# From the third chunk on, VectorE transposes gates, k and q in 32x32 squares

## The chip, the cores and the metric

The kernel runs on one core of a Trainium2 chip. The metric is the device time of one execution in microseconds (us); the time of a kernel is the median of its runs.

## The reference

A gated linear attention (HGRN2) feeds a SwiGLU block. Batch is 4, heads 8, sequence 768, head size 48; the block has 3072 tokens, width 384 and hidden width 1536, all float32.

```python
f = 1.0 / (1.0 + np.exp(-f_logit))
for t in range(S):
    state = f[:, :, t, :, None] * state + np.einsum('bhd,bhe->bhde', k[:, :, t], v[:, :, t])
    y[:, :, t] = np.einsum('bhd,bhde->bhe', q[:, :, t], state)
x = y.transpose(0, 2, 1, 3).reshape(B * S, H * D)
g = x @ w_gate
return (g * (1.0 / (1.0 + np.exp(-g))) * (x @ w_val)) @ w_out
```

## The kernel before

`short_path` does all the work; `general_path` is a second version behind a flag, which runs only when gates become too small. The sequence is cut into six chunks of 128 tokens. A unit is one batch entry of one chunk, so there are 24 units, four to a chunk.

**Attention of a unit** (`attention`, line 453) is a generator whose steps are given out one by one. Tokens arrive on the partitions: f, k and q of 128 tokens and 8 heads lie in `raw` buffers, two for each tensor (lines 332 to 336), each head padded from 48 to 64 columns, so that two heads make 128 columns. The computation wants channels on the partitions and tokens along the free dimension. `transposed` (line 458) therefore has TensorE transpose four 128x128 pieces of a tensor, one for each pair of heads, into one PSUM bank. The steps are:

- f is transposed; ScalarE takes the sigmoid out of PSUM into `gate` (466).
- VectorE scans the gates backwards into `tail` (471), keeps the smallest whole-chunk decay in `least` (474) and prepares `start` (475, 476).
- k and q are transposed; VectorE multiplies k by the tails into `kT` (482), scans forwards into `head` (484) and multiplies q by it into `qT` (486). GpSimd makes the decayed state (490), and `load_after` asks for the unit two further on.
- TensorE forms the scores `sc` (498), VectorE masks them (500), and kT is transposed back into `kt` (505, 507).
- TensorE forms the output `y` from the decayed state (519) and from the scores (522). ScalarE copies it (526), and ten small DMAs on SyncE's queue place it in `xT` (532). `dS` (544) updates the state (550).

**The block** of chunk 0 is a plain product. For chunks 1 to 5, `mlp_seven` (685) does it with Strassen's seven products: first token sums of xT on VectorE, then six `pair` pieces (products on line 715, in four PSUM banks of pool `fps`, whose sums and products VectorE forms on lines 658, 731 and 746), then four down-projection pieces (line 779).

**Order.** `take_turns` gives out the pieces of a chunk's block and between them the 16 attention parts of the next chunk (`attention_steps`, 567). Thus attention of chunks 2 to 5 runs beside the blocks of chunks 1 to 4, and chunk 5's block runs alone. A scheduler then orders each engine's instructions, earlier written first where they are ready; inside a pair TensorE's order is written out (`in_order`). Loads go on SyncE's queue, one DMA each for f, k, q and v of a unit, and so do the copies into xT. SyncE, like the engines, takes its instructions in order. `judge` (946) reduces `least` to the flag that picks the path.

Of the kernel before, what the change touches and what calls it, by code (L numbers as in the profile page):

```python
# [9 lines left out]
FP32 = mybir.dt.float32  # L10
I32 = mybir.dt.int32
U32 = mybir.dt.uint32
AF = mybir.ActivationFunctionType
ALU = mybir.AluOpType
# [5 lines left out]
def general_path(ctx, tc, q, k, v, f_logit, moe_w_gate, moe_w_val, moe_w_out, out):  # L20
# [14 lines left out]
    NCH = S // C  # L35
    HP = H // 2
    W = 64
# [84 lines left out]

    states = [const.tile([128, HP, 2, D], FP32, tag=f"state{i}", name=f"state{i}") for i in range(3)]
    for s in states:
# [7 lines left out]
    def attention(u):  # L132
# [4 lines left out]
        def transposed(dst, src):  # L137
            for a in range(HP):
                nc.tensor.transpose(dst[:, a * C:(a + 1) * C],
                                    src[:, 2 * a:2 * a + 2, :].rearrange("t r d -> t (r d)"), ident)  # L140
# [3 lines left out]
        transposed(p[:, 1], kr)  # L144
        fT = att.tile([128, HP, C], FP32, tag="e1", name="fT")
        nc.scalar.copy(fT, p[:, 0].rearrange("p (a t) -> p a t", t=C))
        kT = att.tile([128, HP, C], FP32, tag="kT", name="kT")
        nc.vector.tensor_copy(kT, p[:, 1].rearrange("p (a t) -> p a t", t=C))
        p = aps.tile([128, 2, 512], FP32, tag="a", name="qTp")
        transposed(p[:, 0], qr)  # L150
        q0 = att.tile([128, HP, C], FP32, tag="q0", name="q0")
        nc.scalar.copy(q0, p[:, 0].rearrange("p (a t) -> p a t", t=C))
# [137 lines left out]
def short_path(ctx, tc, ident, least, judge, q, k, v, f_logit, moe_w_gate, moe_w_val, moe_w_out, out):  # L290
# [9 lines left out]
    nc = tc.nc  # L300
    B, H, S, D = q.shape
    C = 128
    NCH = S // C
    HP = H // 2
    W = 64
# [5 lines left out]
    N1 = C + 1  # L311
    NRAW = 2
    NROT = 2
    assert TB <= 512 and DM % 128 == 0 and D <= W

    const = ctx.enter_context(tc.tile_pool(name="const", bufs=1))
    att = ctx.enter_context(tc.tile_pool(name="att", bufs=1))
# [11 lines left out]
                            pattern=[[1, C]], channel_multiplier=-1)  # L329


    raw = {nm: [const.tile([128, H, W], FP32, tag=f"{nm}raw{i}", name=f"{nm}raw{i}") for i in range(NRAW)]
           for nm in "qkf"}
    for nm in "fkq":
        for t in raw[nm]:
# [3 lines left out]

    gates = [const.tile([128, HP * N1 + 2], FP32, tag=f"gates{i}", name=f"gates{i}") for i in range(NROT)]  # L340
    tails = [const.tile([128, HP * N1 + 2], FP32, tag=f"tails{i}", name=f"tails{i}") for i in range(NROT)]
    start = const.tile([128, HP * N1], FP32, tag="start", name="start")
# [11 lines left out]
    def pairs(t, off=0):  # L354
        return t[:, off:off + HP * N1].rearrange("p (a t) -> p a t", t=N1)
# [17 lines left out]
    units = [(b, c) for c in range(NCH) for b in range(B)]  # L373
    vt = {}

    def load(u):
        b, c = units[u]
        rows = slice(c * C, (c + 1) * C)
        for nm, src in (("f", f_logit), ("k", k), ("q", q)):
            nc.sync.dma_start(out=raw[nm][u % NRAW][:, :, 0:D], in_=src[b, :, rows, :].rearrange("h t d -> t h d"))  # L380
        vt[u] = att.tile([128, H, D], FP32, tag="v", name="v", bufs=4)
        nc.sync.dma_start(out=vt[u], in_=v[b, :, rows, :].rearrange("h t d -> t h d"))
# [67 lines left out]
    def bank(name):  # L450
        return aps.tile([128, 512], FP32, tag="a", name=name)

    def attention(u):
        b, c = units[u]
        fr, kr, qr = (raw[nm][u % NRAW] for nm in "fkq")
        gate, tail = (x[u % NROT] for x in (gates, tails))

        def transposed(name, src):
            p = bank(name)
            for a in range(HP):  # L460
                nc.tensor.transpose(p[:, a * C:(a + 1) * C],  # L461
                                    src[:, 2 * a:2 * a + 2, :].rearrange("t r d -> t (r d)"), ident)
            return p.rearrange("p (a t) -> p a t", t=C)

        p = transposed("fTp", fr)
        nc.scalar.activation(pairs(gate)[:, :, 1:N1], p, AF.Sigmoid)  # L466
        yield


        n = HP * N1  # L470
# [5 lines left out]
        nc.vector.reciprocal(pairs(start)[:, :, 0:1], pairs(start)[:, :, 0:1])  # L476
        yield

        kp = transposed("kTp", kr)
        qp = transposed("qTp", qr)  # L480
        kT = att.tile([128, HP, C], FP32, tag="kT", name="kT")
        nc.vector.tensor_tensor(kT, kp, pairs(tail, 2)[:, :, 0:C], ALU.mult)
        head = att.tile([128, n], FP32, tag="head", name="head", bufs=1)
        nc.vector.tensor_tensor_scan(head, gate[:, 0:n], start, 1.0, op0=ALU.mult, op1=ALU.add)
        qT = att.tile([128, HP, C], FP32, tag="qT", name="qT")
        nc.vector.tensor_tensor(qT, qp, pairs(head)[:, :, 1:N1], ALU.mult)
        if c:
            load_after(u)
            decayed = att.tile([128, HP, 2, D], FP32, tag="decayed", name="decayed")
            nc.gpsimd.tensor_tensor(decayed, states[b], whole.unsqueeze(2).broadcast_to((128, HP, 2, D)), ALU.mult)  # L490
        yield
# [10 lines left out]
        if c < NCH - 1:  # L502
            p = bank("kt")
# [9 lines left out]
        if c:  # L513
# [13 lines left out]
            for h in range(H):  # L527
                f = h * D
                while f < (h + 1) * D:
                    n = min((h + 1) * D, (f // 128 + 1) * 128) - f  # L530
                    r = W * (h % 2) + f - h * D
                    nc.sync.dma_start(out=xT[c][f % 128:f % 128 + n, f // 128, b * C:(b + 1) * C],
                                      in_=yT[r:r + n, h // 2, :])
# [7 lines left out]
        if c < NCH - 1:  # L541
            p = bank("dS")
            for h in range(H):
                nc.tensor.matmul(p[W * (h % 2):W * (h % 2) + W, (h // 2) * D:(h // 2 + 1) * D],  # L544
                                 lhsT=kt[:, h, :], rhs=vt[u][:, h, :], start=True, stop=True)
            dS = p[:, 0:HP * D].rearrange("p (a d) -> p a d", d=D)
            for par in range(2):
                half = slice(W * par, W * par + W)
                if c:
                    nc.vector.tensor_tensor(states[b][half, :, par, :], decayed[half, :, par, :], dS[half], ALU.add)  # L550
                else:
                    nc.scalar.copy(states[b][half, :, par, :], dS[half])
# [3 lines left out]
        if not c:  # L556
            p = bank("xTp")
# [3 lines left out]
        yield  # L561

    def load_after(u):
        if u + NRAW < len(units):
            load(u + NRAW)

    def attention_steps(c):

        runs = [attention(c * B + b) for b in range(B)]
        parts = [1, 2, 1, 2]  # L570
        order = sorted((2 * b + s, b, n) for b in range(B) for s, n in enumerate(parts))
        return [lambda b=b, n=n: [next(runs[b]) for _ in range(n)] for _, b, n in order]
# [284 lines left out]
    for u in range(NRAW):  # L857
        load(u)
    mark = traced[-1]
    keep_warm(5)  # L860
    first = [attention(b) for b in range(B)]
    done = [0] * B

# [6 lines left out]
    fetches.pop(0)()  # L870
    run(0, 0, 1, 2)
    load_after(0)
    for b in range(1, B):
        if b == 1:
            run(1, 0)
            keep_warm(12)
        run(b, 1)
        run(b - 1, 3)
        run(b, 2)
        load_after(b)  # L880
        if b == 1:
            for _ in range(2):
                fetches.pop(0)()
        if b + 1 < B:
            run(b + 1, 0)
        else:
            sizes.pop(0)()
        if b > 1:
            run(b - 2, 5)
        run(b - 1, 4)  # L890
# [31 lines left out]
@with_exitstack  # L922
def kernel(
    ctx: ExitStack,
    tc: tile.TileContext,
    q: bass.AP,
    k: bass.AP,
    v: bass.AP,
    f_logit: bass.AP,
    moe_w_gate: bass.AP,  # L930
    moe_w_val: bass.AP,
    moe_w_out: bass.AP,
    out: bass.AP,
):


    nc = tc.nc
    args = (q, k, v, f_logit, moe_w_gate, moe_w_val, moe_w_out, out)
    HP = q.shape[1] // 2
    flags = ctx.enter_context(tc.tile_pool(name="flags", bufs=1))  # L940
    least = flags.tile([128, HP], FP32, tag="least", name="least")
    ident = flags.tile([128, 128], FP32, tag="idf", name="idf")
    make_identity(nc, ident)
    redo = []

    def judge(bank):
        low = flags.tile([128, 1], FP32, tag="low", name="low")
        nc.vector.tensor_reduce(low, least, axis=mybir.AxisListType.X, op=ALU.min)
        row = bank("row")[0:1, 0:128]
        nc.tensor.transpose(row, low, ident)  # L950
        one = flags.tile([1, 1], FP32, tag="one", name="one")
        nc.vector.tensor_reduce(one, row, axis=mybir.AxisListType.X, op=ALU.min)
        flag = flags.tile([1, 1], I32, tag="flag", name="flag")
        nc.vector.tensor_single_scalar(flag, one, LEAST, op=ALU.is_lt)
        redo.append(nc.values_load(flag[0:1, 0:1], min_val=0, max_val=1,
                                   skip_runtime_bounds_check_because="a comparison"))

    short_path(tc, ident, least, judge, *args)
    with tc.If(redo[0] > 0):
        general_path(tc, *args)  # L960
# [32 lines left out]
```

## Time and profile before

| | |
|---|---|
| median of 3 runs | 671.41 us (671.12 to 671.87) |
| the profiled execution | 671.64 us, its span 669.9 us |
| TensorE busy | 657.1 us (98%) |
| VectorE busy | 443.5 us (66%) |
| ScalarE busy | 191.5 us (29%) |
| GpSimd busy | 22.5 us (3%) |
| TensorE line 461, transposes of f, k and q | 3 x 96 |
| DMA packets | 120667, of them 103712 under 512 bytes |
| moved by DMA | 42.47 MB |

The span is the time from the first to the last instruction in the profiled execution. In lines of the timeline the first number is the start in us from the span's start, the second the length; a line may stand for several instructions that overlap or follow each other (x and a count). The figure in brackets is the engine's idle time before the line and what ended it. In a table by stretch, each engine has its busy time in that stretch. PE is TensorE's matmul, PEld its weight load, DVE VectorE, ACT ScalarE, POOL GpSimd, SPq SyncE's queue.

### The profile page before, as it was taken

Reading aid. Unit: us, or ns where it says so; the run is one execution under the profiler, and the core shown is the slowest. Engines: PE = TensorE matmul, PEld = TensorE weight load, DVE = VectorE, ACT = ScalarE, POOL = GpSimd, SP = SyncE. Lnnn points to the kernel's source line nnn. Section 1 sums busy time; section 2 is a strip of 40 time slices with the busy share of each in tenths; the row PEclk is TensorE's granted clock in tenths of the full one; section 3 lists DMA queues with packets and bytes.
Section 4 is the critical chain, followed back from the end, with each engine's and each line's share of the span. In section 5 each row is a group of like instructions: output and inputs, shape, how many; then the busy total and the mean of one; then the engine's idle time right before and its main releaser. Section 6 shows DMA issues by size and latency. Waiting matters only on the chain.

```text
span 669.9 us, 10567 instructions
## 1 busy us (share of the span) xinstructions
PE 657.1 (98%) x4206; PEld 550.0 (82%) x4206; DVE 443.5 (66%) x765; ACT 191.5 (29%) x284; POOL 22.5 (3%) x38
## 2 busy tenths in 40 slices
PE   7999998999999999999999999999999999999996
PEld 5955555658888999888899888899988898988896
DVE  6889688687778626686843877762587772366631
ACT  2566546203332311323311334131141421111110
POOL 2000000000000000000000000000000000000000
PEclk9999999999999999999999999999999999999999
DMA  9976638113112032121221221212211000100001
GB/s 205 217 196 208 167 106 238 34 24 82 36 36 49 13 64 68 36 48 22 50 46 51 59 48 25 48 28 53 64 39 33 12 1 13 62 1 0 1 1 51
DMA packets 120667, 42.47 MB, mean 63 GB/s; under 512 B 103712, under 2 KB 114464, under 8 KB 120608
## 3 DMA queue, kind: packets, MB, share of 16 engines
q1 hardware_dynamic: 117152, 36.98, 23.7%
q10 hardware_dynamic: 3456, 4.72, 2.0%
q8 instruction: 35, 0.57, 0.4%
q14 instruction: 24, 0.20, 0.1%
HBM read 33.03 MB, written 4.72 MB: 56 GB/s over the span
## 4 chain that ended last, share of the span: by engine, by line
PE 82%; DVE 2%; DMA 1%; issue 0%; ACT 0%; ACTq 0%
PE p L715 31%; PE o L779 21%; PE c L715 12%; PE o L626 4%; PE y L519 3%; PE sc L498 3%; PE y L522 2%; PE kTp L461 1%; PE dS L544 1%; PE kt L505 1%; PE qTp L461 1%; PE fTp L461 1%; DMA w<-in_moe_w_out_dram 1%; DVE top L417 0%; DVE h L618 0%
## 5 line engine op out<-in xcount | busy, mean ns | idle before, releaser
L658 DVE TENSOR_TENSOR rest<-u,p 128x512 f32<-128x512 f32 x90 | 61.8, 687 | 59.8 <-PE p L715 59.6
L779 PE MATMUL o<-w_out,h 128*128 128x192 f32 x480 | 83.6, 329 | 0.0
L779 PEld LDWEIGHTS o<-w_out,h 128*128 128x128 f32 x480 | 77.7, 190 | 2.3 <-issue 1.1
L715 PE MATMUL p<-xT,w_gate 128*128 128x256 f32 x240 | 71.4, 379 | 0.0
L715 PE MATMUL p<-xT,w_val 128*128 128x256 f32 x240 | 71.4, 379 | 0.0
L658 DVE TENSOR_TENSOR u<-u,p 128x512 f32<-128x512 f32 x90 | 61.5, 683 | 5.7 <-PE p L715 1.7
L745 ACT ACTIVATE h<-rest 128x768 f32<-128x768 f32 x30 | 25.3, 843 | 121.5 <-DVE rest L658 121.4
L715 PE MATMUL c<-xT,w_gate 128*128 128x256 f32 x180 | 54.6, 385 | 0.0
L715 PE MATMUL c<-xT,w_val 128*128 128x256 f32 x180 | 53.5, 379 | 0.0
L715 PEld LDWEIGHTS p<-xT,w_val 128*128 128x128 f32 x240 | 45.6, 190 | 6.2
L715 PEld LDWEIGHTS p<-xT,w_gate 128*128 128x128 f32 x240 | 45.6, 190 | 6.2
L658 DVE TENSOR_TENSOR u<-u,o 128x384 f32<-128x384 f32 x15 | 8.3, 555 | 48.9 <-PE o L779 48.9
L715 PEld LDWEIGHTS c<-xT,w_val 128*128 128x128 f32 x180 | 34.2, 190 | 4.6
L471 DVE TENSOR_TENSOR_SCAN tails<-gates,ones 128x516 f32<-128x516 f32 x24 | 29.5, 1230 | 11.9 <-ACT gates L466 11.9
L490 POOL TENSOR_TENSOR decayed<-state,tails 128x384 f32<-128x384 f32 x20 | 19.1, 954 | 532.7 <-DVE state L550 284.8
L715 PE MATMUL p<-xs,sv 128*128 128x256 f32 x120 | 35.8, 380 | 0.0
L715 PE MATMUL p<-xs,sg 128*128 128x256 f32 x120 | 35.7, 379 | 0.0
L500 DVE TENSOR_TENSOR A<-sc,causal 128x512 f32<-128x512 f32 x48 | 31.3, 684 | 5.9 <-PE sc L498 5.8
L522 PE MATMUL y<-A,v 128*48 128x128 f32 x320 | 34.8, 274 | 0.0
L519 PE MATMUL y<-qT,decayed 128*48 128x128 f32 x320 | 34.8, 278 | 0.0
L715 PEld LDWEIGHTS c<-xT,w_gate 128*128 128x128 f32 x180 | 31.5, 190 | 3.9 <-ACT u L723 0.2
L466 ACT ACTIVATE gates<-fTp 128x512 f32<-128x512 f32 x24 | 14.3, 597 | 70.5 <-PE fTp L461 69.5
(117 smaller groups left out, 1116.2 us busy)
## 6 DMA issues: line engine op xcount, KB each, us to landing
fraw<-in_f_logit_dram SPq DMA_DIRECT2D x24, 192.0 KB, 3.0
kraw<-in_k_dram SPq DMA_DIRECT2D x24, 192.0 KB, 3.0
qraw<-in_q_dram SPq DMA_DIRECT2D x24, 192.0 KB, 3.4
v<-in_v_dram SPq DMA_DIRECT2D x24, 192.0 KB, 2.9
w<-in_moe_w_gate_dram SPq DMA_DIRECT2D x6, 768.0 KB, 4.5
w<-in_moe_w_val_dram SPq DMA_DIRECT2D x6, 768.0 KB, 4.5
w<-in_moe_w_out_dram SPq DMA_DIRECT2D x6, 768.0 KB, 5.4
out_dram<-ob ACTq DMA_DIRECT2D x24, 192.0 KB, 2.1
```

Of the source, the lines that this page charges most:

```text
L461: nc.tensor.transpose(p[:, a * C:(a + 1) * C], src[:, 2 * a:2 * a + 2, :].rearrange("t r d -> t (r d)"), ident)
L471: nc.vector.tensor_tensor_scan(tail[:, 0:n][:, ::-1], gate[:, 0:n][:, ::-1], ones[:, ::-1], 1.0, op0=ALU.mult, op1=ALU.add)
L490: nc.gpsimd.tensor_tensor(decayed, states[b], whole.unsqueeze(2).broadcast_to((128, HP, 2, D)), ALU.mult)
L498: nc.tensor.matmul(sc[par][:, a * C:(a + 1) * C], lhsT=kT[r, a, :], rhs=qT[r, a, :], start=True, stop=True)
L500: nc.vector.tensor_tensor(A[:, par], sc[par].rearrange("p (a t) -> p a t", t=C), causal.unsqueeze(1).broadcast_to((128, HP, C)), ALU.mult)
L519: nc.tensor.matmul(y[rows_of(par), cols], lhsT=decayed[:, a, par, :], rhs=qT[:, a, :], start=True, stop=False, skip_group_check=True)
L522: nc.tensor.matmul(y[rows_of(par), cols], lhsT=vt[u][:, 2 * a + par, :], rhs=A[:, par, a, :], start=False, stop=True, skip_group_check=True)
L626: nc.tensor.matmul(p, lhsT=h[n // 2][:, n % 2 * 2 + b // 2, b % 2 * C:(b % 2 + 1) * C], rhs=w_out[:, j, :], start=(n == 0), stop=(n == NF ...
L658: nc.vector.tensor_tensor(dst, a, b, ALU.add)
L715: nc.tensor.matmul(p[:, n, :], lhsT=lhsT, rhs=rhs, start=first and n == 0, stop=last, skip_group_check=True)
L745: nc.scalar.activation(h[j][:, 1:4, :], rest[:, :, 0, :], AF.Silu)
L779: nc.tensor.matmul(p[:, n, :], lhsT=lhsTs[j][:, n * C:(n + 1) * C], rhs=rhs[:, j, :], start=first and j == 0 and n == 0, stop=last and j = ...
```

## The change

For units of chunks 2 to 5 (`c >= SQUARES`), f, k and q are not transposed on TensorE. Instead of one DMA, four bring each tensor in, one for each group of 32 partitions: partition t of a group gets tokens 4t to 4t + 3, all 48 channels, for the four heads of one parity (768 consecutive bytes of a head). For the groups that hold channels 32 to 47 the destination starts 32 columns earlier, so that the same columns hold the wanted 32 channels in all groups; the upper 16 of these are other data, which later steps don't read or meet with zeros. ScalarE takes the sigmoid in place, and VectorE's transpose turns each 32x32 square and writes its 32 tokens with a step of four words. For k and q this goes to `kT` and `qT`, and the products on lines 482 and 486 then work in place there. The two buffers of a tensor become one tile, `rooms`; a squares load takes up most of both, so it is issued only after the transposes of the unit before. Smaller edits keep the padding rows out of the state update and the verdict.

```diff
+    SQUARES = 2
...
-    raw = {nm: [const.tile([128, H, W], FP32, tag=f"{nm}raw{i}", name=f"{nm}raw{i}") for i in range(NRAW)]
+    rooms = {nm: const.tile([128, NRAW * H * W], FP32, tag=f"{nm}raw", name=f"{nm}raw") for nm in "qkf"}
+    raw = {nm: [rooms[nm][:, i * H * W:(i + 1) * H * W].rearrange("t (h d) -> t h d", d=W) for i in range(NRAW)]
            for nm in "qkf"}
...
+    Q = 32
+    NI = C // Q
+    RUN = NI * D
+
+    def squares(nm):
+        return rooms[nm][:, Q:Q + HP * RUN].rearrange("t (a i e) -> t a i e", a=HP, i=NI)[:, :, :, 0:Q]
+
+    def in_turn(t):
+
+        return t.rearrange("p a (t i) -> p a i t", i=NI)
+
     def load(u):
...
         for nm, src in (("f", f_logit), ("k", k), ("q", q)):
+            if c >= SQUARES:
+                for n in range(4):
+                    at = Q * (1 - n % 2)
+                    nc.sync.dma_start(
+                        out=rooms[nm][Q * n:Q * (n + 1), at:at + HP * RUN].rearrange("t (a e) -> t a e", a=HP),
+                        in_=src[b, n // 2::2, rows, :].rearrange("a (t i) d -> t a (i d)", i=NI))
+                continue
...
-        p = transposed("fTp", fr)
-        nc.scalar.activation(pairs(gate)[:, :, 1:N1], p, AF.Sigmoid)
+        if c >= SQUARES:
+            nc.scalar.activation(squares("f"), squares("f"), AF.Sigmoid)
+            nc.vector.transpose(in_turn(pairs(gate)[:, :, 1:N1]), squares("f"))
+        else:
+            p = transposed("fTp", fr)
+            nc.scalar.activation(pairs(gate)[:, :, 1:N1], p, AF.Sigmoid)
...
+        qT = att.tile([128, HP, C], FP32, tag="qT", name="qT")
+        if c >= SQUARES:
+            kp, qp = kT, qT
+            nc.vector.transpose(in_turn(kT), squares("k"))
+            nc.vector.transpose(in_turn(qT), squares("q"))
+            load_after(u)
+        else:
+            kp = transposed("kTp", kr)
+            qp = transposed("qTp", qr)
...
-                half = slice(W * par, W * par + W)
+                half = rows_of(par)
...
     def load_after(u):
-        if u + NRAW < len(units):
-            load(u + NRAW)
+
+        for w, ahead in ((u + 1, True), (u + 2, False)):
+            if w < len(units) and (units[w][1] >= SQUARES) == ahead:
+                load(w)
...
-        nc.vector.tensor_reduce(one, row, axis=mybir.AxisListType.X, op=ALU.min)
+        nc.vector.tensor_reduce(one, row.rearrange("p (n d) -> p n d", n=2)[:, :, 0:D], axis=mybir.AxisListType.XY, op=ALU.min)
```

More of the change, by code (lines that the diff above doesn't have):

```diff
@@ L477, in attention @@
         yield
-        kp = transposed("kTp", kr)
-        qp = transposed("qTp", qr)
         kT = att.tile([128, HP, C], FP32, tag="kT", name="kT")
+        qT = att.tile([128, HP, C], FP32, tag="qT", name="qT")
[7 more added lines that the diff above has]
+            qp = transposed("qTp", qr)
         nc.vector.tensor_tensor(kT, kp, pairs(tail, 2)[:, :, 0:C], ALU.mult)
@@ L484, in attention @@
         nc.vector.tensor_tensor_scan(head, gate[:, 0:n], start, 1.0, op0=ALU.mult, op1=ALU.add)
-        qT = att.tile([128, HP, C], FP32, tag="qT", name="qT")
         nc.vector.tensor_tensor(qT, qp, pairs(head)[:, :, 1:N1], ALU.mult)
         if c:
-            load_after(u)
+            if c < SQUARES:
+                load_after(u)
             decayed = att.tile([128, HP, 2, D], FP32, tag="decayed", name="decayed")
@@ L938 @@
     args = (q, k, v, f_logit, moe_w_gate, moe_w_val, moe_w_out, out)
-    HP = q.shape[1] // 2
+    HP, D = q.shape[1] // 2, q.shape[3]
     flags = ctx.enter_context(tc.tile_pool(name="flags", bufs=1))
```

## The prediction

> **What bounds the kernel now.** I read the page first: its header, the busy shares, the slices and the chain that ended last.
>
> ```profile
> span 669.9 us, 10567 instructions
> ...
> PE 657.1 (98%) x4206; PEld 550.0 (82%) x4206; DVE 443.5 (66%) x765; ACT 191.5 (29%) x284; POOL 22.5 (3%) x38
> ...
> PE   7999998999999999999999999999999999999996
> ...
> PEclk9999999999999999999999999999999999999999
> ...
> PE 82%; DVE 2%; DMA 1%; issue 0%; ACT 0%; ACTq 0%
> ```
>
> TensorE is busy in every slice, at an unreduced granted clock, and the chain runs along it: 82% of the span, against 2% on VectorE. A busy TensorE could still hide waits, so next I read the busy time by stretch: one whole chunk period from its first hidden pair to the next one's, and the last period, in which no attention runs.
>
> ```profile
> core 0: us, PE busy (x) PEld busy (x) DVE busy (x) ACT busy (x) POOL busy (x), PEclk, DMA share, GB/s
> ...
> 259.60:367.50 107.90, 107.90 (x754) 96.96 (x753) 70.50 (x127) 28.57 (x42) 3.33 (x4) 1.00 0.21 45
> ...
> 579.40:669.90 90.50, 84.47 (x432) 77.14 (x431) 44.82 (x81) 12.55 (x21) 0.00 (x0) 0.99 0.04 15
> ```
>
> TensorE is covered for 107.90 of 107.90 us, VectorE for 70.50. In the last period TensorE's busy time is 84.47 us, so four attention units cost the period 107.90 - 84.47 = 23.4 us, 5.9 us a unit. Third, who TensorE's weight loads wait for between 151 and 580 us:
>
> ```profile
> PEld y L519 <- issue: 4.3, 19, 0.3
> ...
> PEld sc L498 <- DVE qT L486: 2.3, 7, 0.3
> ```
>
> The longest entries come to a few us in 428 and none is a single wait over 0.3 us. In the periods that the change touches, TensorE waits for nobody: work taken off it shortens the span, as long as VectorE, which gets the work, doesn't make it wait.
>
> **What leaves TensorE.** Chunks 2 to 5 are 16 units, each with twelve 128x128 transposes (line 461). The timeline gives the distance from one start to the next, which counts where operations overlap:
>
> ```profile
> 259.06 0.60 PE L461 MATMUL fTp<-idf,fraw 128*128 128x128 f32 x4
> ...
> 259.50 0.60 PE L715 MATMUL c<-xT,w_gate 128*128 128x256 f32 x2
> ...
> 269.00 0.60 PE L461 MATMUL kTp<-idf,kraw 128*128 128x128 f32 x4
> ...
> 269.43 0.60 PE L461 MATMUL qTp<-idf,qraw 128*128 128x128 f32 x4
> ...
> 269.87 0.60 PE L715 MATMUL c<-xT,w_gate 128*128 128x256 f32 x2
> ```
>
> Four transposes take 0.44 us, then 0.87 for eight: 1.31 us a unit, 16 x 1.31 = 21.0 us. The four periods' busy time of that line, overlaps counted, is the other bound:
>
> ```profile
> sum 427.60, PE 26.75 PEld 21.96; mean PE 6.69 PEld 5.49
> ```
>
> So the term is -21.0 to -26.8 us. I take -21.6 (1.35 a unit), close to the lower end, because the starts in the timeline are what the next matmul sees; the 0.04 a unit over them stands for the two changes of operands that go as well.
>
> **What VectorE gets.** Three transposes of 128x512 f32 a unit, 48 in all; no such operation is in the trace. The nearest rows are element-wise operations of VectorE with unit stride, by shape and then in sequence:
>
> ```profile
> L658 DVE TENSOR_TENSOR rest<-u,p 128x512 f32<-128x512 f32 x90 | 61.8, 687 | 59.8 <-PE p L715 59.6
> ...
> L658 DVE TENSOR_TENSOR hs<-h 128x256 f32<-128x256 f32 x30 | 12.6, 419 | 0.4
> ```
>
> ```profile
> 269.20 0.69 DVE L658 TENSOR_TENSOR rest<-u,p 128x512 f32<-128x512 f32 x1 [1.04 <-PE p L715]
> 269.80 0.68 DVE L482 TENSOR_TENSOR kT<-kTp,tails 128x512 f32<-128x512 f32 x1
> 270.40 0.68 DVE L486 TENSOR_TENSOR qT<-qTp,head 128x512 f32<-128x512 f32 x1
> ```
>
> An operation of 512 elements lasts 0.69 us and holds the engine 0.60; from 256 to 512 elements it grows by 0.27, or 1.05 ns an element, so 128 elements would last 0.29. I take 0.62 us of engine time for a transpose, the row of the same size. It could come out near 1.2: the transpose writes every fourth word (tokens four to a partition), and a slope of twice 1.05 ns over 512 elements adds 0.54 us. It would also be about that if it were cut into four operations of 128 elements (4 x 0.29 us). So 0.6 to 1.2 us. The Trainium skill's page SBUF — State Buffer, section Door 1: The DMA port swizzle, says that an engine's stream needs two hits to a 16-byte line for full rate and that each access in a new line pays a penalty; by it this write would be on the slow side, and no row of this case shows it. The time that would follow is the second rival, worked out from the rows.
>
> Where does this work lie? The two halves of a period, pairs then down projections, and the fullest stretch I found:
>
> ```profile
> 259.50:331.10 71.60, 71.60 (x460) 62.44 (x459) 54.44 (x94) 22.60 (x33) 2.50 (x3) 1.00 0.20 42
> 331.10:367.50 36.40, 36.40 (x297) 34.62 (x297) 16.16 (x34) 5.96 (x10) 0.83 (x1) 1.00 0.22 50
> ```
>
> ```profile
> 282.00:292.50 10.50, 10.50 (x87) 9.46 (x83) 9.31 (x17) 4.43 (x7) 0.83 (x1) 1.00 0.28 57
> ```
>
> In the down stretch VectorE is 44% busy and hides what comes. The pair stretch holds three units' worth: VectorE goes to 54.4 + 9 x 0.62 = 60.0 us, TensorE to 71.6 - 3 x 1.35 = 67.5, a load of 89%. The 10.5 us stretch has 9.31 / 10.50 = 89% already, and TensorE is covered throughout: such a load can be borne. What a lag costs is seen at the tightest place in that stretch, where, as I count the pairs' four banks, one product must be read before TensorE can begin a later one:
>
> ```profile
> 288.25 0.69 DVE L658 TENSOR_TENSOR u<-u,p 128x512 f32<-128x512 f32 x1
> ```
>
> ```profile
> 289.75 0.59 PE L715 MATMUL p<-xT,sg 128*128 128x256 f32 x2
> ```
>
> The bank is free at 288.94 and wanted at 289.75: 0.81 us to spare. After the change TensorE comes up to 1.35 us earlier and VectorE up to 3 x 0.62 = 1.86 later, so the wait is between nothing and 1.35 + 1.86 - 0.81 = 2.4 us a unit; over 12 units, 0 to 29 us. I take 3 us in all (0.25 a unit), near the lower end, for two rows. Gates no longer wait for TensorE, and ready work is moved forward by the scheduler: the verdict's reduction, written after chunk 4's last step (about 579 us), ran at 548.59. And VectorE has regular gaps to fill:
>
> ```profile
> 548.59 0.16 DVE L948 TENSOR_REDUCE low<-least 128x1 f32<-128x4 f32 x1
> ```
>
> ```profile
> DVE rest L658 <- PE p L715: 46.5, 66, 1.0
> ```
>
> Between 151 and 580 us these are 66 waits of 0.70 us on average, one transpose of 0.62 each.
>
> **The small edits.** The sigmoid takes as many elements from SBUF instead of PSUM; ScalarE is 29% busy, so nothing. Its old reason to wait goes for 16 of 24 units:
>
> ```profile
> ACT gates L466 <- PE fTp L461: 69.5, 15, 11.2
> ```
>
> What is late next for it is the load, and for the transposes VectorE's own queue. The products kT and qT now read two SBUF tensors, and the trace shows what that can cost beside GpSimd:
>
> ```profile
> 261.73 0.83 POOL L490 TENSOR_TENSOR decayed<-state,tails 128x384 f32<-128x384 f32 x1 [26.00 <-DVE tails L471]
> ...
> 262.09 1.56 DVE L484 TENSOR_TENSOR_SCAN head<-gates,start 128x516 f32<-128x516 f32 x1
> ```
>
> ```profile
> 308.60 1.23 DVE L484 TENSOR_TENSOR_SCAN head<-gates,start 128x516 f32<-128x516 f32 x1
> ```
>
> The scan lasts 1.56 us where GpSimd's product starts just before it and 1.23 where none runs: +0.33. At worst each of 16 units pays one such meeting, 5.3 us of VectorE time, and none at best; it counts within the 3 us. The Trainium skill's page SBUF — State Buffer, section SBUF: two separate sides, states that a VectorE operation with two SBUF inputs and a GpSimd operation that reads SBUF exclude each other; the two rows agree.
>
> Loads: twelve DMAs for f, k and q where three were, each row of 768 bytes and every byte twice, and only one unit ahead. SyncE's queue sees it:
>
> ```profile
> 342.25 6.24 SPq L532 DMA_DIRECT2D xT<-yT  x10
> ...
> 349.21 0.53 SPq L380 DMA_DIRECT2D qraw<-in_q_dram  x1
> ...
> 356.00 6.25 SPq L532 DMA_DIRECT2D xT<-yT  x10
> ```
>
> ```profile
> fraw<-in_f_logit_dram SPq DMA_DIRECT2D x24, 192.0 KB, 3.0
> ```
>
> An issue takes 0.62 us, so thirteen take 8.1 and with the ten xT copies 14.3 us of a unit's 26. A load waits for the transposes of the unit before it and then has about a unit's time (103 / 4 = 26 us) to land in 3 us, so I cost it at 0; if that cover went, VectorE, which takes its work in order, would stand behind the missing square. Queued behind the loads are the copies to xT of the chunk's last unit: rival three. Bytes are no limit, since the DMA share of these periods is 0.21 in the row above.
>
> **The sum.** The profiled execution took 671.64 us, 1.74 outside its span and 0.23 over the median of 671.41. 671.64 - 21.6 + 3 = 653.0; less the 0.23, 652.8, rounded **653 us**.
>
> **Rivals.**
> 1. *All hidden, and the switches go too.* No stall at all, and 1.5 us a unit, between the starts (1.31) and the busy time (26.75 / 16 = 1.67): 24 us less, 647 us. For it: TensorE's waits now are near nothing. Against: 89% of VectorE in the pair stretch. Chance 0.10.
> 2. *A transpose holds VectorE 1.2 us.* By every fourth word or a cut into four, as above. The pair stretch then needs 54.4 + 10.8 = 65.2 of 67.5 us. If 89 to 94% of it can be used, 1.7 to 5.1 us a period spill over into TensorE's waits, 7 to 20 us in all: 657 to 670, say 663. Against: every row of 512 elements agrees on 0.69 us. The Trainium skill's line rule, named above, speaks for this rival. Chance 0.22.
> 3. *SyncE's queue delays xT.* Nine more issues ahead of the last unit's copies are 5.6 us; the sums that read xT end at 362.69 and TensorE uses them from 368.39, 5.7 us later:
>
> ```profile
> 362.27 0.42 DVE L661 TENSOR_TENSOR xs<-xT,xs 128x256 f32<-128x256 f32 x1
> ```
>
> ```profile
> 368.39 1.73 PE p L715 x8
> ```
>
> It decides only if the copies slip by more than that, for instance behind a load that waits. As much again in each of four periods is 22 us, the whole gain: up to 671. Against: the queue is free for six us between the issues at 349.21 and at 356.00. Chance 0.05.
> 4. *Slower.* At 1.2 us a transpose and with nothing moved forward, each unit in the pair stretch stalls for 3.6 + 1.35 - 0.81 = 4.1 us at the bank; 12 x 4.1 = 50 us against 21.6 gained, 700 us. It decides from 1.8 us of stall a unit on (21.6 / 12). For it: VectorE is at 89% in the 10.5 us stretch already. Against: the gaps above. Chance 0.08.
>
> **How the numbers follow.** The forecast has 0.55; its own range is 649 to 658. 647 takes in rival 1; up to 667 it takes in most of rival 2, leaving out rival 4 (0.08), most of rival 3 and some quarter of rival 2: 0.08 + 0.04 + 0.06 = 0.18. Faster by over 0.2% (1.3 us, about what a measurement can tell) gets the forecast, rival 1, nearly all of rival 2 and some of 3: 0.87; within 0.2% 0.05; slower 0.08.
>
> **What would show it.** Right: line 461 has 96 transposes in all instead of 288; periods of about 103 us from pair to pair; VectorE transposes of about 0.7 us; TensorE covered for over 98% in the touched periods. Wrong: transposes over 1 us; waits of the pair's products for VectorE's line 658 of several us a period; waits of the token sums for xT; or TensorE's order so changed that periods shorten by less though no wait appears.

## The result and the profile after

The changed kernel takes 652.21 us (652.13 to 652.40, four runs) against 671.64 us (671.12 to 672.25, four runs): a ratio of 0.9711 with a 95% interval of 0.9694 to 0.9728, or 19.4 us less. The forecast was 653. Line numbers have moved: TensorE's pair products are on 752 (715 before), its down projections on 816 (779), VectorE's sums on 695 (658), and the transposes of chunks 0 and 1 on 485 (461).

The page of the changed kernel, header, busy shares and chain:

```profile
span 650.6 us, 10425 instructions
...
PE 638.0 (98%) x4014; PEld 530.3 (82%) x4014; DVE 480.1 (74%) x813; ACT 194.4 (30%) x286; POOL 27.6 (4%) x38
...
PE 96%; DVE 3%; issue 0%; ACT 0%; DVEq 0%
```

TensorE has 192 instructions less and 19.1 us of busy time less, VectorE 48 instructions more and 36.6 us more, and the bound has not moved: the chain still runs along TensorE. Next, busy time by stretch: a chunk's pairs, its down projections, both together, and the last period without attention.

```profile
253.52:321.90 68.38, 68.38 (x422) 58.87 (x422) 53.79 (x92) 23.96 (x33) 2.23 (x2) 1.00 0.24 63
321.90:356.93 35.03, 35.03 (x286) 33.28 (x285) 26.00 (x47) 7.09 (x11) 2.50 (x2) 1.00 0.29 74
253.52:356.93 103.41, 103.41 (x706) 92.15 (x706) 79.80 (x138) 31.05 (x44) 4.72 (x4) 1.00 0.26 67
...
559.40:650.60 91.20, 84.66 (x434) 77.42 (x432) 44.97 (x81) 11.27 (x20) 0.00 (x0) 0.99 0.04 15
```

A period is 103.4 us (107.9 before) and TensorE is still covered throughout. Read the VectorE column against the prediction's two stretches: the pair stretch has 53.8 us where it had 54.4, the down stretch 26.0 where it had 16.2. VectorE's new work went to the stretch with room. The new operations themselves:

```profile
L511 DVE STREAM_TRANSPOSE kT<-kraw 128x512 f32<-128x512 f32 x16 | 18.0, 1122 | 0.0
L512 DVE STREAM_TRANSPOSE qT<-qraw 128x512 f32<-128x512 f32 x16 | 17.8, 1116 | 7.9 <-PE y L554 7.5
L491 DVE STREAM_TRANSPOSE gates<-fraw 128x512 f32<-128x512 f32 x16 | 17.5, 1093 | 0.1
```

They last 1.1 us, not 0.7; where another operation stands right behind one, that one starts some 0.97 us later, where 0.62 was reckoned. TensorE nevertheless waits for VectorE only here between 149 and 559 us (matmul first, weight load second):

```profile
PE p L752 <- DVE u L695: 0.5, 1, 0.5
```

```profile
PEld p L752 <- DVE u L695: 0.9, 1, 0.9
```

Where the 19.3 us of span went is read from the chain, at the first pair of chunk 1's block and of chunk 5's. Before, then after:

```profile
151.80 0.87 PE c L715 x4
...
579.40 0.86 PE c L715 x4
```

```profile
149.54 0.86 PE c L752 x4
```

```profile
559.59 0.87 PE c L752 x4
```

The four touched periods shrink from 427.6 to 410.05 us, 17.55 less. Another 2.26 us are gained ahead of them, which the prediction did not have, and the last period gives back 0.5.

The 17.55 us are less than TensorE's transposes were worth. By the distances between starts, they held 21.5 us of the four periods before, and the matmuls that stayed take 3.9 us more after: 1.9 in the pairs' products, 1.6 in the scores and outputs, 0.5 in the down projections. Hardly any of it shows as standing still: TensorE is covered for 409.5 of the 410.05 us. The loss lies in many small steps between matmuls, and since the profile models where a matmul ends, waits that short could hide in them; what lengthens them was not found out.

### The profile page after: what moved, and what is told of

It is laid out like the page before. It is cut to its first block, busy times and chain, and to the rows that moved or that the text cites. A ratio compares the mean times of both kernels' runs of the same rounds, so it can differ in the third digit from the quotient of the medians.

```text
span 650.6 us, 10425 instructions
## 1 busy us (share of the span) xinstructions
PE 638.0 (98%) x4014; PEld 530.3 (82%) x4014; DVE 480.1 (74%) x813; ACT 194.4 (30%) x286; POOL 27.6 (4%) x38
## 4 chain that ended last, share of the span: by engine, by line
PE 96%; DVE 3%; issue 0%; ACT 0%; DVEq 0%
PE p L752 31%; PE o L816 22%; PE c L752 12%; PE o L663 5%; PE val L639 5%; PE gate L639 5%; PE sc L533 4%; PE y L554 3%; PE y L557 3%; PE kt L540 2%; PE dS L579 2%; PE y L572 1%; PE fTp L485 1%; PE qTp L485 0%; PE kTp L485 0%
## 5 line engine op out<-in xcount | busy, mean ns | idle before, releaser
L525 POOL TENSOR_TENSOR decayed<-state,tails 128x384 f32<-128x384 f32 x20 | 24.2, 1210 | 508.6 <-DVE state L585 198.0
L783 DVE TENSOR_TENSOR h<-h,rest 128x768 f32<-128x768 f32 x30 | 28.6, 955 | 12.8 <-ACT h L782 12.8
L557 PE MATMUL y<-A,v 128*48 128x128 f32 x320 | 36.7, 275 | 0.0
L554 PE MATMUL y<-qT,decayed 128*48 128x128 f32 x320 | 36.2, 278 | 0.0
L760 ACT COPY u<-c 128x512 f32<-128x512 f32 x30 | 17.4, 581 | 50.9 <-DMA fraw<-in_f_logit_dram 24.6
```

Source lines behind the costliest of these rows:

```text
L554: nc.tensor.matmul(y[rows_of(par), cols], lhsT=decayed[:, a, par, :], rhs=qT[:, a, :], start=True, stop=False, skip_group_check=True)
L557: nc.tensor.matmul(y[rows_of(par), cols], lhsT=vt[u][:, 2 * a + par, :], rhs=A[:, par, a, :], start=False, stop=True, skip_group_check=True)
L783: nc.vector.tensor_tensor(h[j][:, 1:4, :], h[j][:, 1:4, :], rest[:, :, 1, :], ALU.mult)
```

## The experiments

Two theories are compared in most of them. By the first, TensorE's time is all that counts and VectorE's new work is hidden, moved into gaps by the scheduler. By the second, that work costs a good part, and TensorE's saving is larger than thought or is partly a freedom from waits. Ratios are to the kernel before on the same chip.

**TensorE's transposes added again.** Twelve transposes of a constant a unit, into banks that nobody reads.

```diff
+        def idle_transposes(name):
+            p = bank(name)
+            for a in range(HP):
+                nc.tensor.transpose(p[:, a * C:(a + 1) * C], causal, ident)
...
             nc.vector.transpose(in_turn(pairs(gate)[:, :, 1:N1]), squares("f"))
+            idle_transposes("fi")
...
             nc.vector.transpose(in_turn(qT), squares("q"))
+            idle_transposes("ki")
+            idle_transposes("qi")
```

> The changed kernel with the twelve 128x128 transposes of a unit left on TensorE as well, of a constant, into banks that nobody reads; they stand where the old ones stood. VectorE's work stays. Theory one, the gain is TensorE's time: it comes back whole, 21 to 24 us, 673 to 676 us, more than the kernel before. Rival, part of the gain is the freedom from waiting on PSUM banks and on TensorE: below 670.

673.65 us, ratio 1.0024 (1.0014 to 1.0034). Against the changed kernel's 0.9711 that is 0.0313, 21.0 us (21.4 by the medians). With the intervals of the two ratios it is 19.7 to 22.3. The first theory held: TensorE's transposes are worth about 1.31 us a unit, the distance between starts in the trace of before, and the whole gain goes with them.

**VectorE's transposes added to the kernel before.**

```diff
+        def idle_transpose(t):
+            if c >= 2:
+                nc.vector.transpose(t.rearrange("p a (t i) -> p a i t", i=4),
+                                    ones[:, 0:HP * C].rearrange("p (a i e) -> p a i e", a=HP, i=4))
...
+        idle_transpose(pairs(tail)[:, :, 1:N1])
...
+        idle_transpose(kT)
...
+        idle_transpose(qT)
```

> The kernel before with VectorE's three transposes a unit added (of a constant, into kT, qT and the tails before these are written); TensorE's stay. VectorE gets 16 x 3 x 1.1 = 53 us more and nothing is taken away. Theory one, such work is hidden when it can be moved: 0 to 6 us more, 672 to 678 us. Rival, VectorE's time counts in the pair stretch, three units of 3.3 us in each of four periods: up to 40 us more, 690 to 712.

674.01 us, ratio 1.0045 (1.0028 to 1.0063): 53 us of VectorE work, counted by the lengths of the operations (its busy time, overlaps counted once, is 39 us up), cost 3.0 us, between 1.9 and 4.2. The rival that counts it in the pair stretch would have needed 18 or more.

**VectorE's transposes issued twice** in the changed kernel.

```diff
             nc.vector.transpose(in_turn(pairs(gate)[:, :, 1:N1]), squares("f"))
+            nc.vector.transpose(in_turn(pairs(gate)[:, :, 1:N1]), squares("f"))
...
+            nc.vector.transpose(in_turn(kT), squares("k"))
+            nc.vector.transpose(in_turn(qT), squares("q"))
```

> The changed kernel with each of VectorE's transposes issued twice in a row: 53 us more of VectorE work, nothing else. A period of 103.4 us has VectorE busy for 79.8; with 12 x 1.1 more it is 93, 90%. Theory one, the scheduler spreads it over the period: 652 to 662 us. Rival, the pair stretch fills up (53.8 of 68.4 us now, up to 10 more): TensorE waits for banks, 670 to 690.

657.82 us, ratio 0.9782 (0.9765 to 0.9799): 5.6 us by the medians, 4.8 by the ratios, for another 53 of VectorE. The table by stretch shows where they went, pairs first:

```profile
254.00:323.00 69.00, 67.97 (x413) 58.44 (x412) 55.70 (x92) 23.96 (x33) 2.49 (x2) 1.00 0.26 68
323.00:358.50 35.50, 35.50 (x296) 33.19 (x295) 33.84 (x60) 7.09 (x11) 1.67 (x2) 1.00 0.26 65
```

The pair stretch takes 1.9 us of it, the down stretch 7.8 and is at 33.8 of 35.5 us. That room is nearly used up, and TensorE now stands still for 1.0 us of the pair stretch (67.97 of 69.00).

**Tokens written side by side.** The squares' tokens come out in the wrong order, so this kernel computes the attention of chunks 2 to 5 on permuted tokens.

```diff
-        return t.rearrange("p a (t i) -> p a i t", i=NI)
+        return t.rearrange("p a (i t) -> p a i t", i=NI)
```

> The changed kernel with VectorE's transposes writing each square's 32 tokens side by side instead of every fourth word; loads as they are, so tokens come out in the wrong order and the attention of chunks 2 to 5 is computed on permuted tokens. On the transpose: if the step of four words makes it 1.11 us, it falls to about 0.7; if the transpose itself runs at that rate, it stays at 1.1. On the time: theory one, VectorE's work is hidden in its gaps and TensorE sets the period: 650 to 652 us, although VectorE does about 19 us less. Rival, the longer transposes already cost part of the gain: 640 to 648.

```profile
L511 DVE STREAM_TRANSPOSE kT<-kraw 128x512 f32<-128x512 f32 x16 | 11.2, 702 | 0.0
```

The transpose falls from 1.12 to 0.70 us, so the step of the write is the cause. The time is 652.26 us, ratio 0.9707 (0.9690 to 0.9723): 19 us less of VectorE work by the lengths (15 of busy time) bring nothing that can be measured.

**Tokens two to a partition.** Loads in half chunks of two tokens a run; the write then steps two words.

```diff
-        return t.rearrange("p a (t i) -> p a i t", i=NI)
+        return t.rearrange("p a (j t i) -> p a j i t", j=2, i=2)
...
-                for n in range(4):
+                for n, j in [(n, j) for n in range(4) for j in range(2)]:
                     at = Q * (1 - n % 2)
+                    half = slice(c * C + 64 * j, c * C + 64 * j + 64)
                     nc.sync.dma_start(
-                        out=rooms[nm][Q * n:Q * (n + 1), at:at + HP * RUN].rearrange("t (a e) -> t a e", a=HP),
-                        in_=src[b, n // 2::2, rows, :].rearrange("a (t i) d -> t a (i d)", i=NI))
+                        out=rooms[nm][Q * n:Q * (n + 1), at:at + HP * RUN].rearrange("t (a j e) -> t a j e", a=HP, j=2)[:, :, j],
+                        in_=src[b, n // 2::2, half, :].rearrange("a (t i) d -> t a (i d)", i=2))
```

> The changed kernel with tokens two to a partition in each half of a chunk: eight loads a tensor of 384-byte rows instead of four of 768, and the transposes write every second word. Computes the same. If what costs is only that each word falls into a 16-byte line of its own, two words now share one and the transpose falls to about 0.7 us; if any step costs, it stays near 1.1; between is a share. On the time: theory one 650 to 653 us. Rival, SyncE's queue: 25 issues of 0.62 us and ten copies are 21.7 us of a unit's 26, so copies into xT come late and it is 655 to 665.

714.55 us, ratio 1.0629 (1.0611 to 1.0647), far beyond either expectation of the time. The transpose shortens:

```profile
L512 DVE STREAM_TRANSPOSE kT<-kraw 128x512 f32<-128x512 f32 x16 | 11.2, 699 | 0.0
```

At two words a step it is as fast as at one. The loss is elsewhere. Who SyncE's queue and TensorE waited for, one such wait in the queue, and the stretch behind it, in which TensorE stands still:

```profile
SPq L568 <- DMA out_dram<-ob: 38.7, 6, 17.6
```

```profile
PE sc L534 <- DVE qT L521: 39.5, 6, 14.4
PE p L753 <- DVE xs L699: 10.8, 4, 9.2
```

```profile
345.56 24.56 SPq L568 DMA_DIRECT2D xT<-yT  x10
370.22 4.55 SPq L401 DMA_DIRECT2D fraw<-in_f_logit_dram  x8
```

```profile
372.00:388.00 16.00, 2.01 (x17) 1.82 (x17) 7.49 (x13) 3.07 (x4) 0.83 (x1) 0.59 0.42 91
```

Six times, for up to 17.6 us, SyncE stood before a copy into xT until an output store had landed (and seven more times before a load, 40.5 us in all). What stands behind such a copy in the queue is late with it: here the next unit's loads, issued from 370.22 on. Without them there is no qT, and TensorE waited 14.4 us for its scores and was busy for 2.0 of 16 us. The token sums, which read xT, made it wait less, 10.8 us against 39.5. Is that the number of issues? The next run has as many.

**Eight loads a tensor**, cut by heads, with rows, squares and transposes of the changed kernel.

```diff
-                for n in range(4):
+                for n, j in [(n, j) for n in range(4) for j in range(2)]:
...
-                        out=rooms[nm][Q * n:Q * (n + 1), at:at + HP * RUN].rearrange("t (a e) -> t a e", a=HP),
-                        in_=src[b, n // 2::2, rows, :].rearrange("a (t i) d -> t a (i d)", i=NI))
+                        out=rooms[nm][Q * n:Q * (n + 1), at:at + HP * RUN].rearrange("t (a e) -> t a e", a=HP)[:, 2 * j:2 * j + 2],
+                        in_=src[b, n // 2 + 4 * j:n // 2 + 4 * j + 3:2, rows, :].rearrange("a (t i) d -> t a (i d)", i=NI))
```

> The changed kernel with each of a tensor's four loads cut in two by heads, so 24 loads of 768-byte rows a unit; squares, transposes and everything else as in the changed kernel. The run with tokens two to a partition took 714.6 us with transposes of 0.70 us. If the number of issues on SyncE's queue is why, this run is about as slow, 700 to 720 us, though its bytes and rows are those of the changed kernel. If the shorter rows or the other order of squares is why, it stays at 652 to 660.

656.43 us, ratio 0.9777 (0.9760 to 0.9795). Twelve more issues a unit, each of half the size, cost 4.2 us; the number of issues alone is not why the other run took 714.6. In this trace no copy into xT waits for an output store, and one load does, for 0.4 us. What makes a copy wait for a store there was not found out: the order in which the scheduler put them differs in that run, and no run separates it from the shorter rows.

**f on TensorE, k and q on VectorE.**

```diff
-            if c >= SQUARES:
+            if c >= SQUARES and nm != "f":
...
-        if c >= SQUARES:
-            nc.scalar.activation(squares("f"), squares("f"), AF.Sigmoid)
-            nc.vector.transpose(in_turn(pairs(gate)[:, :, 1:N1]), squares("f"))
-        else:
-            p = transposed("fTp", fr)
-            nc.scalar.activation(pairs(gate)[:, :, 1:N1], p, AF.Sigmoid)
+        p = transposed("fTp", fr)
+        nc.scalar.activation(pairs(gate)[:, :, 1:N1], p, AF.Sigmoid)
```

> The changed kernel with f loaded, transposed and put through the sigmoid as before, on TensorE and from PSUM; k and q in squares on VectorE. Theory one: a third of TensorE's saving is lost, 16 x 0.44 = 7 us, 659 us, and VectorE's 18 us less bring nothing. Rival, gates that no longer wait for TensorE are what lets work move forward: without it more is lost, 663 to 670.

661.92 us, ratio 0.9844 (0.9825 to 0.9862), between the two. 0.0133 more than the changed kernel is 8.9 us, of which a third of TensorE's 21 is 7. The rest, 1.9 us, is hardly more than the noise of the two ratios (1.7). Such waits as the changed kernel has once are here in greater number:

```profile
PEld p L748 <- DVE u L691: 6.1, 8, 2.0
```

VectorE has some 18 us less to do here and yet holds TensorE up more often. That the gates wait for TensorE again is a likely reason, but this run changes f's loads too and does not show it.

**VectorE in the written order**, in the changed kernel and in the kernel before.

```diff
+        begin = traced[-1]
         take_turns(pieces, attention_steps(c + 1) if c + 1 < NCH else [], 2 if c else 8)
+        if 1 <= c < NCH - 1:
+            in_order(begin, (mybir.EngineType.DVE,))
```

> The changed kernel with VectorE's instructions held to the order in which they are written during the blocks of chunks 1 to 4, so that nothing is moved forward. Theory two, moving forward hides the transposes: without it the pair stretch has 54.4 + 9 x 1.1 = 64.3 us of work in 67.5, and each of its 12 units waits 2 to 4 us: 676 to 700 us. Rival, the gaps at the written places suffice: 652 to 660.

> The kernel before with VectorE's order held to the written one in the same stretch: the control of the run above. If the kernel before hardly moves work forward, since its gates wait for TensorE, it stays within 1% of 671.5 us, and the pinned pair shows what the change brings without that freedom. If it slows by as much as the changed kernel, the written order is bad by itself and says nothing of the transposes.

748.79 us for the changed kernel, ratio 1.1119 (1.1088 to 1.1150), and 721.74 for the one before, 1.0662 (1.0573 to 1.0750). The control is bad by itself, contrary to its expectation of 1%, but not as bad: held to the written order the change costs 27 us (31 by the ratios) instead of bringing 19. The pair has its limits: the control's runs lie between 712 and 726 us, and the granted clock is down in both, to 0.98 in the control and 0.94 in the changed kernel, so that the 27 us are waits and slower matmuls together. The place was not a bank, as I had it, but the scores. TensorE's waits for qT, changed kernel first:

```profile
PE sc L533 <- DVE qT L520: 56.5, 13, 4.7
```

```profile
PE sc L498 <- DVE qT L486: 28.4, 13, 2.8
```

The chain of the changed kernel in written order shows why: the unit's operations stand one behind the other ahead of the scores.

```profile
162.72 1.15 DVE tails L499
...
164.35 0.97 DVE kT L511
165.32 0.91 DVE qT L512
...
166.75 1.14 DVE head L519
...
168.66 2.08 PE sc L533 x16
```

**Loads one unit ahead, nothing else**, on the kernel before, for the 2.26 us ahead of the first touched period.

```diff
-        if u + NRAW < len(units):
-            load(u + NRAW)
+        for w, ahead in ((u + 1, True), (u + 2, False)):
+            if w < len(units) and (units[w][1] >= 2) == ahead:
+                load(w)
```

> The kernel before with nothing changed but when loads are asked for: those of chunks 2 to 5 one unit ahead instead of two. In the trace of before, the third unit of chunk 1 loads k and q ahead of the last weight pieces in SyncE's queue, and TensorE later waits 1.74 us for a product that stands behind those weights; in the changed kernel that wait is gone. If the order of loads is why, about 669.5 to 670 us; if not, 671.5, or more where a load comes late.

669.92 us, ratio 0.9979 (0.9971 to 0.9988), 1.4 us less. TensorE's one long wait of the kernel before,

```profile
116.98 3.49 PE L626 MATMUL o<-w_out,h 128*128 128x384 f32 x10 [1.74 <-DVE h L618]
```

is gone, and the first pair of chunk 1's block stands at 149.80 in the chain instead of 151.80. In SyncE's queue the loads of k and q stood ahead of three pieces of w_out, issued from 100.59 on; now one piece goes out ahead of k and one ahead of q, from 99.40 on, and the last piece follows at 108.92 instead of 111.36.

**Squares from chunk 1 on**, with tokens four and two to a partition.

```diff
-    SQUARES = 2
+    SQUARES = 1
```

> The changed kernel with squares from chunk 1 on: four more units, 48 transposes less on TensorE. TensorE's share is 4 x 1.35 = 5.4 us: 647 us if VectorE has room beside chunk 0's block. But there VectorE is busy 78 of 90 us (it joins the weights' halves) and gets 13 us more, and weights, loads and copies share SyncE's queue: 652 to 660 if that decides.

> The same with tokens two to a partition. If transposes are shorter so, VectorE has some 5 us more room beside chunk 0's block and this is up to 3 us faster than the run above; if SyncE's queue, with 25 issues a unit beside 18 weight pieces, decides, it is slower by 2 to 10 us.

675.00 us, ratio 1.0044 (1.0026 to 1.0061), and 740.37, 1.1023 (1.1006 to 1.1041): both worse than their counterparts, by 23 and 26 us, more than expected. The second, expected within 10 us of the first, is 65 us behind it and has the waits for output stores of the other run with tokens two to a partition. In the first, the time is lost before the first pair:

```profile
176.99 0.59 PE L752 MATMUL c<-xT,w_gate 128*128 128x256 f32 x2
```

That is 27 us later than in the changed kernel. In this stretch TensorE and ScalarE wait for weights and their halves:

```profile
ACT up L430 <- DMA w<-in_moe_w_val_dram: 9.9, 1, 9.9
...
PEld o L663 <- DVE w_out L442: 7.0, 3, 4.0
```

Whether VectorE's 13 us more or the queue that weights and squares share comes first was not separated. No version tried that computes the same beats the changed kernel.

## Why the prediction was right

**TensorE's term** was right: -21.6 forecast, -21.0 (19.7 to 22.3) by the run with the transposes added again. The distance between starts was the right measure, and the busy time with its overlaps (26.8) was not.

**The price of a transpose** is the term that was mis-sized. I took a length of 0.69 and 0.62 us of engine time from the row of equal size; a transpose lasts 1.11 and holds the engine 0.97 (from 276.07 to 277.04 below). That is nearer to my second rival's 1.2, and for a reason given there, the write to every fourth word: with the write side by side or every second word it lasts 0.70. The rule of the Trainium skill's page SBUF — State Buffer, section Door 1: The DMA port swizzle, that two accesses should share a 16-byte line, agrees with all three lengths; I should have weighed it above the row with unit stride.

**The second rival's time** (657 to 670) did not come, because the step "the pair stretch holds three units' worth" was wrong. It was to go from 54.4 to 60.0 us of VectorE and stayed at 53.8. I had the reason in hand, ready work is moved forward, but used it only to choose a small stall. In the changed kernel it decides where the work stands. Of the twelve transposes of a period seven stand in the pair stretch and five among the down projections, together with the two scans of two units, where the kernel before had those of one. From the timeline of VectorE after the change, the end of the down projections:

```profile
344.88 1.11 DVE L512 STREAM_TRANSPOSE qT<-qraw 128x512 f32<-128x512 f32 x1
...
348.01 1.23 DVE L499 TENSOR_TENSOR_SCAN tails<-gates,ones 128x516 f32<-128x516 f32 x1 [0.73 <-POOL decayed L525]
349.16 1.21 DVE L519 TENSOR_TENSOR_SCAN head<-gates,start 128x516 f32<-128x516 f32 x1
```

And the gates are ready long before their scan; from the pair stretch, with GpSimd's line:

```profile
262.09 1.08 DVE L491 STREAM_TRANSPOSE gates<-fraw 128x512 f32<-128x512 f32 x1
...
276.07 1.11 DVE L512 STREAM_TRANSPOSE qT<-qraw 128x512 f32<-128x512 f32 x1 [0.99 <-PE y L554]
...
277.04 0.70 DVE L585 TENSOR_TENSOR state<-decayed,dS 48x192 f32<-48x192 f32 x2
277.77 0.69 DVE L520 TENSOR_TENSOR qT<-qT,head 128x512 f32<-128x512 f32 x1
277.91 1.25 POOL L525 TENSOR_TENSOR decayed<-state,tails 128x384 f32<-128x384 f32 x1 [33.35 <-PE c L752]
279.19 1.23 DVE L499 TENSOR_TENSOR_SCAN tails<-gates,ones 128x516 f32<-128x516 f32 x1 [0.73 <-POOL decayed L525]
```

No tails scan stands between 262.09 and 279.19. That this freedom suffices is shown by the transposes issued twice (some 5 us for 53). That it is needed is what the pinned pair speaks for (27 us lost instead of 19 gained), though the written order costs the kernel before 50 us as well and holds back all of VectorE's work, not the transposes alone.

**The stall term** was right in size by luck: 3 us forecast against 3.0 (1.9 to 4.2) for the work alone, but built from the wrong price and the wrong place, and in the changed kernel the loss is no stall. TensorE stands still there for 0.5 us in the touched periods, and the rest is the longer steps between its matmuls. Of the signs of being wrong, transposes over 1 us came true, and periods that shorten by less though no wait appears in part: the four periods shorten by 17.55 us where the two terms leave 18.6. **A gain was missed**: 1.4 us from the order of loads, which I costed at nothing. That the time came out within 1 us of the forecast owes something to it: TensorE's term was 0.6 us too large, and the missed gain more than made up for that.

The parts add up: -21.0, +3.0 and -1.4 are -19.4 us, as measured. They were run separately, and each is known to about 1 us, so the sum says no more than that the parts do not act on each other by much above 2 us.

**The third rival**, SyncE's queue delaying xT, did not show in the changed kernel, whose token sums wait no more than before; the run with tokens two to a partition shows that queue as a limit, at 714.6 us, but by late loads more than by late copies into xT. **The fourth** is the pinned run: slower once nothing is moved forward, at the scores instead of the bank. **The small edits**: the scan forward no longer meets GpSimd's product (1.22 us on average, 1.34 before), but the scan backward now waits for it, eight times for up to 0.73 us, as in the rows above, and GpSimd's product itself lasts 1.25 us there where it lasted 0.83. In these rows it starts 0.14 us after the product qT, which now has both inputs in SBUF. The exclusion that the Trainium skill's page SBUF — State Buffer, section SBUF: two separate sides, states agrees with the longer product. The scan's wait is another thing: the profile puts it down to a signal of GpSimd's product, an order that the program sets. Neither is on TensorE's path.

## What to carry to other kernels

Here work that moved from a saturated engine to one with gaps was worth the first engine's time between starts, less a few us, as the second could do it early: look at what gates its first step, and at the next stretch with room, more than at the load of the stretch where the code has it. A write with a step of four words costs engine time that a step of one or two does not (1.11 us against 0.70); where that engine is not short of time, as here, it is not worth more transfers. A load rule changed in passing can move other transfers in the same queue, so compare the stretches that the change does not touch.

## What the runs showed of the hardware that was not expected

A VectorE transpose of 128x512 float32 lasts 0.70 us when it writes every word or every second word, and 1.11 us when it writes every fourth.

Where TensorE waited, the rows show a lower granted clock, and the work after a wait was slower. In the stretch of 372 to 388 us above, with 2.0 of 16 us busy, it is 0.59. In the changed kernel in written order, sixteen score matmuls take 2.08 us after a wait of several us (the chain above) and 1.09 us where TensorE was busy ahead of them:

```profile
259.90 1.09 PE sc L533 x16
```

So its period is 129.8 us instead of 103.4, of which only a part is waiting: TensorE stands still for 14.6 us, and its work takes 115.2 us instead of 103.4, at a granted clock of 0.92.

```profile
149.20:279.00 129.80, 115.23 (x718) 100.74 (x717) 82.07 (x140) 32.95 (x48) 3.33 (x4) 0.92 0.24 63
```

A wait on TensorE was paid for a second time here, by the slower work, which the prediction's price of a stall did not contain.
